# Three short moves in the opening of a fused attention-and-gated-MLP kernel

## The chip, the cores and the metric

The kernel runs on one core of a Trainium2 chip. Its metric is the device time in microseconds (us) of that core. A core has several engines that run side by side, each working through its own list of instructions in order: TensorE (PE in the profile, with its weight loads as PEld), VectorE (DVE), ScalarE (ACT), GpSimd (POOL) and SyncE (SP), which here issues every transfer (DMA). An engine waits for another through semaphores. TensorE writes only into PSUM, of which this kernel uses eight banks; a bank must be emptied by ScalarE or VectorE before TensorE may fill it again.

## The reference, cut to what matters

The input x has 2048 tokens of width 640. It is normalised once, and two branches read the result: a linear attention of 32 heads of width 20 and a gated MLP of width 1536.

```python
xn = (x - mean) / sqrt(var + 1e-5)
q, k, v = split(xn @ wqkv)                       # 32 heads of 20
pq, pk = q @ w_phi[h], k @ w_phi[h]              # per head
phi_q = concat(softmax(pq), softmax(-pq)); phi_k = concat(softmax(pk), softmax(-pk))
kv = phi_k.T @ v; z = sum(phi_k)
o = (phi_q @ kv) / (phi_q @ z + 1e-6)
out = x + o @ wo + (silu(xn @ w1) * (xn @ w3)) @ w2
```

## The kernel before, in words

Tokens are cut into 16 tiles of 128. `xnT` holds the normalised x transposed, the form in which TensorE needs it. The whole order is written out by hand: the kernel is a list of calls, and each engine gets its instructions in the order in which the calls come. This document is about the opening, the calls from line 683 to line 814; after them come 16 turns of `phi_unit` for k, then 20 turns for q with the output.

**Normalisation.** `stats(t, 2)` (L644) gives VectorE four `bn_stats` (L223) and two `bn_aggr` (L226) for two tiles, and GpSimd a chain of six small instructions (L233, L236, L255 to L261) that makes 1/sqrt(var) in `rstd`. `lx(t, 2)` (L649) has VectorE apply it (L265), and `by_dma(t)` (L677) has SyncE transpose a tile into `xnT` (L678). Tiles 0, 1 and 3 are transposed by TensorE instead (`T`, `by_pe`: five transposes at L283 into a bank, two copies by ScalarE at L287).

**Raw V.** For tiles 0 to 3 the product with V's weights starts before their statistics are there: `raw_part` (L294) multiplies unnormalised x. The result is emptied from PSUM with the factor `rstd`: `raw_scaled` does it on ScalarE in two activations (L305), `raw_scaled_dve` on VectorE in two `tensor_scalar` (L312). The rest of V comes from `V(t)`: ten matmuls (L344), three copies by ScalarE (L359).

**MLP units.** `unit()` makes ten matmuls of 512 columns, five for the gate (gp, weights w1) and five for up (weights w3), and ScalarE's tanh (L455). It returns a function which, when called, has VectorE form the two products: `gs` (L472), which frees the gate's bank, and the one into `reg_h` (L475), which frees up's. The units of the opening are g0 to g7. g0 and g1 are done in halves of 256 columns (`glu_half`, L461), since tiles 2 and 3 come later than 0 and 1. "Unit seven" is g6, the seventh of them.

**Fused weights.** k is never formed: `FB(d)` (L669) multiplies a chunk of k's weights, which SyncE has brought in transposed (`ldT`, L138), with phi's weights (`fuse`, six matmuls at L428, two copies by ScalarE at L437). phi's weights are first spread into blocks, `wphi`, by one VectorE product (`phi_blocks`, L419).

**PSUM.** Six banks are handed out singly (`bank`), in the order in which they come free; two form a pair (`two`). A call that takes a bank waits until the instructions that read its last content are done. Before the change `FB` takes the pair for even d and two single banks for odd d.

Of the kernel before, what the change touches and what calls it, by code (L numbers as in the profile page):

```python
# [12 lines left out]
def kernel(  # L13
# [17 lines left out]
    nc = tc.nc  # L31
# [3 lines left out]
    ALU = mybir.AluOpType  # L35
    AX = mybir.AxisListType

    _, S, D = A_x.shape
# [13 lines left out]
    CH = 6 * 3 * Dh  # L52
# [16 lines left out]
    def bank(name, dt=f32):  # L69
        n = 512 if dt == f32 else 1024  # L70
        return psum.tile([P, n], dt, name=name, tag="bank")
# [6 lines left out]
    wkphi = one.tile([P, KD, D], bf, name="wkphi")  # L78
# [17 lines left out]
    wkT, wqT, wv = w_nat[:, 0], w_nat[:, 1], w_nat[:, 2]  # L96
# [19 lines left out]
    v_raw = one.tile([P, RAW, D], f32, name="v_raw")  # L116
# [7 lines left out]
    def ld(dst, src):  # L124
        nc.sync.dma_start(out=dst, in_=src)  # L125
# [9 lines left out]
    with tc.manual_schedule():  # L135
        def ldT(dst, i, d):
            rows = slice(d * P, (d + 1) * P)
            nc.sync.dma_start_transpose(  # L138
                out=dst[:, :, rows], in_=A_wqkv[rows, i * D : (i + 1) * D]
            )  # L140
# [3 lines left out]
        def ld_tiles(t, n):  # L144
            ld(
                xin[:, (t // 4) % 3, t % 4 : t % 4 + n],
                x2[t * P : (t + n) * P, :].rearrange("(t p) d -> p t d", p=P),
            )
# [7 lines left out]
        for c in range(KD):  # L156
# [15 lines left out]
            out=mask[:], in_=mask[:], pattern=[[8, KD], [-20, 8]], base=0,  # L172
# [3 lines left out]
            out=mask[:], in_=mask[:], pattern=[[-8, KD], [20, 8]], base=19,  # L176
# [7 lines left out]
            out=own[:], in_=own[:], pattern=[[-64, 2], [-20, 3]], base=0,  # L184
# [3 lines left out]
            out=own[:], in_=own[:], pattern=[[64, 2], [20, 3]], base=19,  # L188
# [26 lines left out]
        rstd = one.tile([P, NST], f32, name="rstd")  # L215

        def ln_stats(*ts):
            made = []
            for t in ts:
                xt = xin[:, (t // 4) % 3, t % 4, :]  # L220
                st = work.tile([P, 2, 6], f32, name="st")
                for i in range(2):
                    nc.vector.bn_stats(out=st[:, i, :], in_=xt[:, i * HD : (i + 1) * HD])  # L223
                made.append(st)
            for t, st in zip(ts, made):
                nc.vector.bn_aggr(out=mv[:, t, :], in_=st[:])  # L226
# [4 lines left out]
        def ln_pow(t, n):  # L231
            r = slice(t, t + n)
            nc.gpsimd.tensor_scalar(  # L233
                out=ve[:, r], in0=mv[:, r, 1], scalar1=EPS, scalar2=None, op0=ALU.add
            )
            nc.gpsimd.tensor_tensor(out=ry[:, r], in0=ve[:, r], in1=mhalf[:, 0:n], op=ALU.pow)  # L236
# [8 lines left out]
        def ln_newton(t, n):  # L245

            r = slice(t, t + n)
            eng = nc.gpsimd
            if n == 1:
                eng.tensor_scalar(  # L250
                    out=rstd[:, r], in0=ry[:, r], scalar1=ve[:, r], scalar2=ry[:, r],
                    op0=ALU.mult, op1=ALU.mult,
                )
            else:
                eng.tensor_mul(out=rstd[:, r], in0=ry[:, r], in1=ry[:, r])  # L255
                eng.tensor_mul(out=rstd[:, r], in0=rstd[:, r], in1=ve[:, r])
            eng.tensor_scalar(
                out=rstd[:, r], in0=rstd[:, r], scalar1=-0.5, scalar2=1.5,
                op0=ALU.mult, op1=ALU.add,
            )  # L260
            eng.tensor_mul(out=rstd[:, r], in0=rstd[:, r], in1=ry[:, r])  # L261

        def ln_x(t):
            xt = xin[:, (t // 4) % 3, t % 4, :]
            nc.vector.tensor_scalar(  # L265
                out=xt, in0=xt, scalar1=mv[:, t, 0:1], scalar2=rstd[:, t : t + 1],
                op0=ALU.subtract, op1=ALU.mult,
            )
# [34 lines left out]
        def raw_scaled(t, ps):  # L303
            for i, (a, b) in enumerate(((0, CH), (CH, D))):
                nc.scalar.activation(  # L305
                    out=v_raw[:, t, a:b], in_=ps[i][:, 0 : b - a],
                    func=AF.Identity, scale=rstd[:, t : t + 1],
                )

        def raw_scaled_dve(t, ps, i):  # L310
            a, b = ((0, CH), (CH, D))[i]
            nc.vector.tensor_scalar(  # L312
                out=v_raw[:, t, a:b], in0=ps[i][:, 0 : b - a],
                scalar1=rstd[:, t : t + 1], scalar2=None, op0=ALU.mult,
            )

        def column_sum(c):
            junk = work.tile([P, D], bf, name="junk")
# [16 lines left out]
        def tile_of(t):  # L335
            return slice(t * P, (t + 1) * P)
# [81 lines left out]
        def phi_blocks():  # L418
            nc.vector.tensor_mul(  # L419
                out=wphi[:],  # L420
                in0=wps[:, :, None, :].to_broadcast([P, KD, 8, Dh]),
                in1=mask[:, :, :, None].to_broadcast([P, KD, 8, Dh]),
            )

        def fuse(dst, wT, d, ps):

            for b, c, h0, h1 in PARTS:
                nc.tensor.matmul(  # L428
                    ps[b][:, Dh * (h0 - 16 * b) : Dh * (h1 - 16 * b)],
                    wT[:, c, d * P : (d + 1) * P],  # L430
                    wphi[:, c, h0 - 6 * c : h1 - 6 * c, :],
                    start=((b, c) in ((0, 0), (1, 2))),
                    stop=((b, c) in ((0, 2), (1, 4))),
                    skip_group_check=True,
                )
            for b in range(2):
                nc.scalar.copy(out=dst[:, d, b * HD : (b + 1) * HD], in_=ps[b][:, 0:HD])  # L437

        def glu_unit(sc, fi, banks=None):

            gp, up = banks or (bank("gp")[:], bank("up")[:])
            for ps, w in ((gp, w1), (up, w3)):
                for c in range(KD):
                    nc.tensor.matmul(  # L444
                        ps,
                        w[:, c, fi * P : (fi + 1) * P],
                        xnT[:, c, sc * 512 : (sc + 1) * 512],
                        start=(c == 0),
                        stop=(c == KD - 1),
                    )  # L450
            return glu_done(sc, fi, gp, up)
# [6 lines left out]
        def glu_half(i, w, sc, fi, ps):  # L458

            for c in range(KD):  # L460
                nc.tensor.matmul(  # L461
                    ps[:, i * 256 : (i + 1) * 256],
                    w[:, c, fi * P : (fi + 1) * P],
                    xnT[:, c, sc * 512 + i * 256 : sc * 512 + (i + 1) * 256],
                    start=(c == 0),
                    stop=(c == KD - 1),
                    skip_group_check=True,
                )
# [175 lines left out]
        def stats(t0, n):  # L644
            ln_stats(*range(t0, t0 + n))
            ln_pow(t0, n)
            ln_newton(t0, n)

        def lx(t0, n):  # L649
            if t0 < BY_DMA:  # L650
                nc.vector.reciprocal(out=rstd[:, t0 : t0 + n], in_=ry[:, t0 : t0 + n])
            for t in range(t0, t0 + n):
                ln_x(t)
# [3 lines left out]
        T = x_transposed  # L657

        def unit(banks=None):
            return glu_unit(*glu.pop(0), banks)  # L660

        def two(name):
            both = pair(name)
            return both[:, 0], both[:, 1]

        def V(t, ps=None):
            v_unit(vaug[:, t], tile_of(t), ps)

        def FB(d):  # L669
            if d % 2:  # L670
                ps = [bank("pf"), bank("pf")]
            else:
                ps = two("pf")
            fuse(wkphi, wkT, d, ps)


        def by_dma(t):  # L677
# [12 lines left out]
        vps = [two("v0"), [bank("pv"), bank("pv")]]  # L690
# [26 lines left out]
        ld_glu(256, 512)  # L717
        ld_tiles(8, 2)
        ld_tiles(10, 2)
        raw_scaled(1, vps[1])  # L720
        lx(3, 1)
        raw_scaled_dve(0, vps[0], 0)
        raw_scaled_dve(0, vps[0], 1)
        ps2 = [bank("pv"), bank("pv")]
        for c in range(KD):
            raw_part(2, c, ps2)
        ps3 = [bank("pv"), bank("pv")]
        for c in range(KD):
            raw_part(3, c, ps3)
        T(3)  # L730
        (sc, fa), (_, fb) = glu.pop(0), glu.pop(0)
        ga, ua = two("g0")
        glu_half(0, w1, sc, fa, ga)
        raw_scaled(2, ps2)
        raw_scaled(3, ps3)
        gb = bank("gp")[:]
# [49 lines left out]
        by_dma(12)  # L786
        by_dma(13)
        V(8)
        stats(14, 2)
        V(9, two("pv"))  # L790
        phi_blocks()
        V(10)
        V(11, two("pv"))
        ldT(wkT, 1, 2)
        lx(14, 2)
        by_dma(14)
        by_dma(15)
        ldT(wkT, 1, 3)
        ldT(wkT, 1, 4)
        g6 = unit()  # L800
        FB(0)
        g6()
        V(12)
        FB(1)
        ld_glu(512, F)
        nc.sync.dma_start_transpose(out=wqT, in_=A_wqkv[:, 0:D])
        V(13)
        g7 = unit()
        g7()
        FB(2)  # L810
        V(14)
        FB(3)
        FB(4)
        V(15)

# [111 lines left out]
```

## Time and profile before

| what | value |
|---|---|
| median of 3 runs | 270.81 us (270.58 to 270.89) |
| the profiled execution's own time | 270.84 us |
| its span, first to last instruction | 269.1 us |
| TensorE busy | 262.1 us, 97% |
| VectorE, ScalarE, GpSimd busy | 192.6, 115.2, 91.9 us |
| TensorE's granted clock | full speed in every slice |

The span is 1.7 us shorter than the execution's time; that rest lies around the program. In a row of the timeline stand the start, the length, the engine, the line, the operation with its output and inputs, how many instructions were merged, and in brackets how long the engine had been idle before and for whom. Matmuls are pipelined: each row's length contains the last matmul's run through the array, so that the distance from one start to the next tells what a group costs.

### The profile page before, as it was taken

Reading aid. Unit: us, or ns where it says so; the run is one execution under the profiler, and the core shown is the slowest. Engines: PE = TensorE matmul, PEld = TensorE weight load, DVE = VectorE, ACT = ScalarE, POOL = GpSimd, SP = SyncE. Lnnn points to the kernel's source line nnn. Section 1 sums busy time; section 2 is a strip of 40 time slices with the busy share of each in tenths; the row PEclk is TensorE's granted clock in tenths of the full one; section 3 lists DMA queues with packets and bytes.
Section 4 is the critical chain, followed back from the end, with each engine's and each line's share of the span. In section 5 each row is a group of like instructions: output and inputs, shape, how many; then the busy total and the mean of one; then the engine's idle time right before and its main releaser. Section 6 shows DMA issues by size and latency. Waiting matters only on the chain.

```text
span 269.1 us, 5283 instructions
## 1 busy us (share of the span) xinstructions
PE 262.1 (97%) x1977; PEld 167.2 (62%) x1996; DVE 192.6 (72%) x360; ACT 115.2 (43%) x350; POOL 91.9 (34%) x89
## 2 busy tenths in 40 slices
PE   8999998999999999999999999999999999999994
PEld 6666565655555555555555555677777777777773
DVE  4698964297777777779997789977667777776341
ACT  5774455745566665435665555422222222221000
POOL 5052530064333333424543333333344444333000
PEclk9999999999999999999999999999999999999999
DMA  6988555995000000060000296556554655556831
GB/s 182 254 229 171 101 121 100 345 199 94 0 0 2 0 1 3 1 173 0 0 2 0 54 307 74 120 139 148 130 136 119 151 129 127 140 140 129 153 97 55
DMA packets 67660, 29.11 MB, mean 108 GB/s; under 512 B 54576, under 2 KB 66224, under 8 KB 67632
## 3 DMA queue, kind: packets, MB, share of 16 engines
q1 hardware_dynamic: 67632, 28.74, 45.2%
q8 instruction: 17, 0.28, 0.4%
q14 instruction: 11, 0.09, 0.2%
HBM read 13.13 MB, written 2.62 MB: 59 GB/s over the span
## 4 chain that ended last, share of the span: by engine, by line
PE 83%; DVE 9%; POOL 3%; DMA 2%; issue 2%; SPq 1%; DVEq 0%
PE acc L583 27%; PE up L444 16%; PE gp L444 16%; PE pq L344 8%; PE pk L344 8%; DVE st L223 3%; PE pr L520 2%; PE pkv L485 2%; DMA reg_h<-in_A_x_dram 2%; DVE reg_h L265 2%; DVE reg_h L475 2%; PE pv L344 2%; DVE gs L472 1%; SPq L125 1%; POOL ry L236 1%
## 5 line engine op out<-in xcount | busy, mean ns | idle before, releaser
L410 POOL TENSOR_TENSOR phi<-phi,rk 128x1320 bf16<-128x1320 bf16 x32 | 77.3, 2414 | 130.6 <-DVE rk L409 96.9
L444 PEld LDWEIGHTS <-w 128*128 128x128 bf16 x460 | 43.5, 98 | 48.3 <-DMA w<-in_B_w_dram 0.5
L407 DVE TENSOR_REDUCE sk<-phi 128x66 f32<-128x1320 bf16 x32 | 48.8, 1527 | 30.7 <-ACT phi L373 29.6
L444 PE MATMUL up<-xnT,w 128*128 128x512 bf16 x226 | 56.8, 379 | 0.3
L444 PE MATMUL gp<-xnT,w 128*128 128x512 bf16 x215 | 56.0, 378 | 0.7
L583 PE MATMUL acc<-reg_v,reg_h 128*128 128x320 bf16 (+2 forms) x384 | 54.9, 299 | 0.0
L344 PEld LDWEIGHTS <-xnT 128*128 128x128 bf16 x440 | 41.8, 98 | 19.9 <-issue 1.1
L373 ACT ACTIVATE phi<-pq 128x360 bf16<-128x360 f32 (+2 forms) x96 | 24.8, 364 | 58.0 <-issue 53.9
L583 PEld LDWEIGHTS <-reg_h 128*128 128x128 bf16 x384 | 37.3, 98 | 14.4
L455 ACT ACTIVATE th<-gp 128x512 f32<-128x512 f32 x47 | 28.3, 602 | 30.0 <-PE gp L444 29.5
L475 DVE SCALAR_TENSOR_TENSOR reg_h<-gs,up 128x512 bf16<-128x512 bf16 x47 | 32.3, 688 | 5.2 <-DVE gs L472 0.5
L373 ACT ACTIVATE phi<-pk 128x360 bf16<-128x360 f32 (+2 forms) x96 | 24.8, 364 | 20.7 <-PE pk L344 20.7
L472 DVE SCALAR_TENSOR_TENSOR gs<-th,gp 128x512 bf16<-128x512 f32 x47 | 30.9, 658 | 3.2 <-ACT th L455 3.2
L592 DVE TENSOR_TENSOR res<-acc,xr 128x320 bf16<-128x320 f32 (+2 forms) x32 | 14.3, 487 | 19.8 <-PE acc L583 19.8
L583 PE MATMUL acc<-reg_w,reg_v 128*128 128x320 bf16 (+2 forms) x160 | 24.5, 299 | 0.0
L344 PE MATMUL pk<-wkphi,xnT 128*128 128x360 bf16 (+1 forms) x160 | 24.3, 299 | 0.0
L344 PE MATMUL pq<-wqphi,xnT 128*128 128x360 bf16 (+1 forms) x160 | 24.3, 299 | 0.0
L409 DVE RECIPROCAL rk<-sk 128x66 f32<-128x66 f32 x32 | 18.1, 567 | 3.2
L583 PEld LDWEIGHTS <-reg_v 128*128 128x128 bf16 x160 | 15.7, 98 | 6.1
L344 PE MATMUL pv<-reg_w,xnT 128*128 128x360 bf16 x120 | 17.4, 299 | 0.8 <-DVE reg_h L475 0.5
L223 DVE BATCH_NORM_STATS2 st<-reg_h 128x6 f32<-128x320 bf16 x32 | 13.4, 477 | 4.2 <-DMA reg_h<-in_A_x_dram 4.2
L541 DVE TENSOR_TENSOR o__77<-pr,den 128x360 bf16<-128x360 f32 (+1 forms) x32 | 14.2, 486 | 0.6
(79 smaller groups left out, 159.0 us busy)
## 6 DMA issues: line engine op xcount, KB each, us to landing
w<-in_B_w_dram SPq DMA_DIRECT2D x2, 1280.0 KB, 8.7
xr<-in_A_x_dram SPq DMA_DIRECT2D x16, 160.0 KB, 2.5
out_dram<-res SPq DMA_DIRECT2D x15, 160.0 KB, 1.8
reg_h<-in_A_x_dram SPq DMA_DIRECT2D x6, 320.0 KB, 4.5
reg_v<-in_B_w_dram SPq DMA_DIRECT2D x1, 1920.0 KB, 8.8
w<-in_B_w_dram SPq DMA_DIRECT2D x4, 320.0 KB, 4.7
reg_w<-in_A_wqkv_dram SPq DMA_DIRECT2D x5, 160.0 KB, 3.8
reg_w<-in_A_wo_dram SPq DMA_DIRECT2D x1, 800.0 KB, 7.7
```

Source lines behind the costliest of these rows:

```text
L223: nc.vector.bn_stats(out=st[:, i, :], in_=xt[:, i * HD : (i + 1) * HD])
L344: nc.tensor.matmul(ps[i][:, 0 : b - a], xnT[:, c, cols], w[:, c, a:b], start=(c == 0), stop=(c == KD - 1), skip_group_check=True,)
L373: nc.scalar.activation(out=dst[:, c0 : c0 + n, g, 0:k], in_=p.rearrange("p (c f) -> p c f", c=n), func=AF.Exp, scale=1.0 - 2.0 * g,)
L407: nc.vector.reduce_sum(out=sk[:], in_=rows, axis=AX.X)
L409: nc.vector.reciprocal(out=rk[:], in_=sk[:])
L410: nc.gpsimd.tensor_mul(out=rows, in0=rows, in1=rk[:, :, :, None].to_broadcast([P, 2 * NCH, 3, Dh]))
L444: nc.tensor.matmul(ps, w[:, c, fi * P : (fi + 1) * P], xnT[:, c, sc * 512 : (sc + 1) * 512], start=(c == 0), stop=(c == KD - 1),)
L455: nc.scalar.activation(out=th[:], in_=gp, func=AF.Tanh, scale=0.5)
L472: nc.vector.scalar_tensor_tensor(out=gs[:], in0=th[:], scalar=1.0, in1=gp, op0=ALU.add, op1=ALU.mult)
L475: nc.vector.scalar_tensor_tensor(out=hT[:, 4 * sc : 4 * sc + 4, fi, :], in0=gs[:].rearrange("p (t s) -> p t s", t=4), scalar=0.5, in1=up.r ...
L583: nc.tensor.matmul(ps[:, 0 : b - a], rows[j][0], rows[j][1][:, a:b], start=(j == 0), stop=(j == len(rows) - 1),)
L592: nc.vector.tensor_tensor(out=res[:, a:b], in0=ps[:, 0 : b - a], in1=xr[:, a:b], op=ALU.add)
```

## The change

1. `raw_scaled_dve` goes. Raw V of tile 0 is now emptied by ScalarE (`raw_scaled(0, vps[0])`), ahead of tile 1's. VectorE has two instructions less there, ScalarE two more.
2. `T(3)`, the transposes of tile 3 on TensorE, moves behind the first half of g0's gate.
3. `phi_blocks` moves ahead of `stats(14, 2)` and of `V(9)`.
4. g6 and its products move ahead of `lx(14, 2)` and of the transposes of tiles 14 and 15. `ldT(wkT, 1, 3)` moves ahead of those transposes as well.
5. `FB` always takes the pair. `FB(2)` moves ahead of g7, and `FB(3)` ahead of `V(14)`, so that no two `FB` follow each other directly.

```diff
-        def raw_scaled_dve(t, ps, i):
-            a, b = ((0, CH), (CH, D))[i]
-            nc.vector.tensor_scalar(
-                out=v_raw[:, t, a:b], in0=ps[i][:, 0 : b - a],
-                scalar1=rstd[:, t : t + 1], scalar2=None, op0=ALU.mult,
-            )
...
         def FB(d):
-            if d % 2:
-                ps = [bank("pf"), bank("pf")]
-            else:
-                ps = two("pf")
-            fuse(wkphi, wkT, d, ps)
+            fuse(wkphi, wkT, d, two("pf"))
...
+        raw_scaled(0, vps[0])
+        lx(3, 1)
         raw_scaled(1, vps[1])
-        lx(3, 1)
-        raw_scaled_dve(0, vps[0], 0)
-        raw_scaled_dve(0, vps[0], 1)
...
-        T(3)
         (sc, fa), (_, fb) = glu.pop(0), glu.pop(0)
         ga, ua = two("g0")
         glu_half(0, w1, sc, fa, ga)
+        T(3)
         raw_scaled(2, ps2)
...
         V(8)
+        phi_blocks()
+        V(9, two("pv"))
         stats(14, 2)
-        V(9, two("pv"))
-        phi_blocks()
         V(10)
         V(11, two("pv"))
         ldT(wkT, 1, 2)
+        ldT(wkT, 1, 3)
+        g6 = unit()
+        g6()
         lx(14, 2)
         by_dma(14)
         by_dma(15)
-        ldT(wkT, 1, 3)
         ldT(wkT, 1, 4)
-        g6 = unit()
         FB(0)
-        g6()
         V(12)
         FB(1)
         ld_glu(512, F)
         nc.sync.dma_start_transpose(out=wqT, in_=A_wqkv[:, 0:D])
         V(13)
+        FB(2)
         g7 = unit()
         g7()
-        FB(2)
+        FB(3)
         V(14)
-        FB(3)
         FB(4)
         V(15)
```

## The prediction

> **What bounds the kernel.** I read the page's busy shares and slices first.
>
> ```profile
> span 269.1 us, 5283 instructions
> PE 262.1 (97%) x1977; PEld 167.2 (62%) x1996; DVE 192.6 (72%) x360; ACT 115.2 (43%) x350; POOL 91.9 (34%) x89
> PEclk9999999999999999999999999999999999999999
> ```
>
> TensorE is busy from end to end at full clock, so a change can only gain where TensorE stands still. Second, whom TensorE waited for, whole span:
>
> ```profile
> PE idle L200 <- DVE nought L196: 1.1, 1, 1.1
> PE pv L344 <- DVE reg_h L475: 0.5, 1, 0.5
> PE v L294 <- DMA reg_w<-in_A_wqkv_dram: 0.4, 1, 0.4
> PE pv L344 <- DVE gs L472: 0.3, 1, 0.3
> PE g L461 <- DVE v_raw L312: 0.2, 1, 0.2
> ```
>
> That is the whole list. The change touches three of these: the two pv waits and the g wait. From 43 us to the end the same view is empty, so what TensorE gains by then should reach the end. Third, the timeline of TensorE around the pv waits:
>
> ```profile
> 39.00 0.48 PE L428 MATMUL pf<-wphi,reg_w 128*128 128x140 bf16 x6
> 39.32 1.52 PE L344 MATMUL pv<-reg_w,xnT 128*128 128x360 bf16 x10
> 40.67 0.48 PE L428 MATMUL pf<-wphi,reg_w 128*128 128x140 bf16 x6
> 41.48 0.31 PE L344 MATMUL pv<-reg_w,xnT 128*128 128x360 bf16 x1 [0.33 <-DVE gs L472]
> 42.27 1.37 PE L344 MATMUL pv<-reg_w,xnT 128*128 128x280 bf16 x9 [0.48 <-DVE reg_h L475]
> 43.47 1.24 PE L444 MATMUL gp<-xnT,w 128*128 128x512 bf16 x5
> ```
>
> By starts, an FB costs 0.32 (39.00 to 39.32) and a V 1.35 (39.32 to 40.67). FB(1) and V(13) should take 1.67 and took 2.80 (40.67 to 43.47). V(13) was handed g6's two banks, and VectorE freed them late. Why late, fourth, from VectorE, GpSimd and SyncE:
>
> ```profile
> 28.89 0.22 POOL L233 TENSOR_SCALAR ve<-mv 128x2 f32<-128x2 f32 x1 [3.57 <-DVE mv L226]
> ...
> 37.08 0.94 DVE L419 TENSOR_TENSOR wphi<-wps,mask 128x800 bf16<-128x800 bf16 x1
> 37.25 0.84 POOL L233 TENSOR_SCALAR ve<-mv 128x2 f32<-128x2 f32 x1 [4.04 <-DVE mv L226]
> ...
> 40.03 0.80 DVE L265 TENSOR_SCALAR reg_h<-reg_h,mv,rstd 128x640 bf16<-128x640 bf16 x2 [2.01 <-POOL rstd L261]
> 40.74 0.68 DVE L472 SCALAR_TENSOR_TENSOR gs<-th,gp 128x512 bf16<-128x512 f32 x1
> 41.53 0.69 DVE L475 SCALAR_TENSOR_TENSOR reg_h<-gs,up 128x512 bf16<-128x512 bf16 x1
> ```
>
> VectorE idled 2.01 us for GpSimd's rstd of tiles 14 and 15, with g6's products queued behind, although their tanh had ended at 38.72. Fifth, the g wait at 12.85 and the next wait for weights:
>
> ```profile
> 12.85 0.71 PE L461 MATMUL g<-xnT,w 128*128 128x256 bf16 x5 [0.19 <-DVE v_raw L312]
> ...
> 17.32 0.76 PEld L444 LDWEIGHTS <-w 128*128 128x128 bf16 x5 [0.22 <-DMA w<-in_B_w_dram]
> ```
>
> **The change part by part.**
>
> *g6's products ahead of lx(14).* They start after the tanh, at 38.8, and take 1.48 as before (40.74 to 42.22): done by 40.28. V(13)'s turn on TensorE comes at 40.67 + 0.32 = 40.99, so even g6's own banks are free, by 0.7. With FB(1) on the pair V(13) takes an older set, V(10)'s, copied out by 36.4. Gain: 2.80 - 1.67 = **1.13**.
>
> *phi_blocks ahead of stats(14).* The statistics end 0.87 later (0.94 less the overlap with its neighbour), so GpSimd starts at 38.12. Its chain took 2.12 when ve took 0.22 (28.89 to 31.01) and 2.75 beside wphi (37.25 to 40.00); at 38.12 wphi is done, so I take 2.12: rstd at 40.24, against 40.00. lx(14) follows there, when g6's products are just over, 0.24 later than before. FB(0), which reads wphi, stands at 39.00. The Trainium skill (SBUF — State Buffer, Who interferes with whom) says that a VectorE instruction with two SBUF inputs contends with a GpSimd instruction that reads SBUF. The trace agrees: ve stood 0.84, up to wphi's end, and POOL's other waits before a ve (3.57) left it at 0.22. Without that rule 2.75 would stand, and the transfers below would come 0.63 later, a cost of up to 0.7.
>
> *SyncE.* ldT(2) was issued at 38.05; ldT(3) now follows, to 40.64. The transpose of tile 14 starts 0.24 later than its 40.50, at 40.74, tile 15's at 42.03, ldT(4) at 43.31 (was 44.39). Tiles land 2.4 after issue, so 14 and 15 lie in xnT at 43.2 and 44.5; V(14) and V(15) read them at 45.1 and 46.8. ldT's took 2.8 to 3.2 to land, so chunk 4 is there at 46.1 to 46.5. The later loads of w1 and w3 start about 0.4 earlier.
>
> *FB on the pair.* Each FB now waits for ScalarE's copies of the one before. New starts on TensorE: FB(1) 40.67, V(13) 40.99, FB(2) 42.34, g7 (2.16) 42.66, FB(3) 44.82, V(14) 45.14, FB(4) 46.49, V(15) 46.81. FB(0)'s copies ended at 40.27. FB(1)'s ended at 42.24 and follow V(12)'s, which do not move: 0.1 before FB(2). FB(2)'s and FB(3)'s have 2 and 1 us. FB(4)'s binding wait is chunk 4: cost 0 to 0.06. Before, that chunk held FB(4) by 0.03 (landed 47.62, due 47.63 with its load ahead, started 47.66). I take 0 now, a gain of 0.03; the upper end is 0.7 if SyncE runs as late as in the sentence on 2.75.
>
> *Raw V of tile 0 on ScalarE, T(3) moved.* Two activations cost 0.93 (the row at 10.91 for tile 1), VectorE sheds 1.00. ScalarE empties tile 0 by 11.84, before TensorE wants the pair, at 12.22. Five transposes take 0.27, so g could have begun at 12.49 and began at 12.85: 0.36 lost before. The eight halves of 0.545 then end at 16.85 instead of 17.21. But g2's w1 landed at 17.28 and it began at 17.32; its load was issued behind tile 2's transpose, and nothing ahead of it on SyncE moves. So the 0.36 becomes a wait for w1: gain **0**. It would be a gain if w1 landed earlier.
> ScalarE itself: tile 3's copies start 0.48 after its transposes, at 13.25 instead of 12.70, so tiles 2 and 3 and the table load run 0.55 later and g0's tanh ends at 17.69. VectorE took it up at 17.60, so its first product is 0.15 late; lx(6) had waited to 19.09 for rstd, 0.08 past the product's end and a usual 0.08 of overlap, which covers it. That rstd comes 0.6 earlier, since the statistics of 4 and 5 start 0.95 sooner and those of 6 and 7 at their landing, 13.95. If the cover fails, 0.55 goes down VectorE's chain to lx(10): tile 10 landed at 33.9 and V(10) began at 34.12, so the cost is at most 0.35. A loss is not excluded; I take 0.
> The transposes of tiles 4 and 5 go out 1 us earlier, at 16.4, while w3's quarter is landing (18.31, wanted 18.41). Landings followed the order of issue throughout the opening, so I take 0. Upper end: their 320 KB ahead of w3 at the window's 243 GB/s, 1.3 less 0.1 slack, 1.2.
>
> **Sum.** 1.13 + 0.03 + 0 = 1.16. The profiled execution took 270.84, 0.03 over the median: 269.68, and 269.65 beside the median; I say **269.7**, or 0.4% faster.
>
> **The rivals.**
> 1. *Part of it comes back*: chunk 4 late at FB(4), or VectorE's lateness at V(10). Their margins, 0 and 0.2, are the smallest here; against it stands that both shifts come out near zero. Cost 0.2 to 0.7: 269.9 to 270.4.
> 2. *The opening gains too.* The profile names VectorE's v_raw as what released tile 2's transpose on SyncE, whose issue took 2.25 against the usual 1.2. If removing v_raw shortened it by 1.0, w1 would land at 16.3 and 0.4 more could be won, of which V(10)'s tile leaves 0.2: 269.4. Against: that issue began at 11.29, right when its input was ready, and 640 KB issued before it were landing until 13.95. The Trainium skill (the same section) says that DMA never contends with a compute engine except through GpSimd's descriptors; by it this rival falls, and no other row here shows it.
> 3. *No change*: w3 comes late by the 1.2 above, and TensorE waits at 18.4 what it wins at 41: 270.9.
> 4. *Slower: the round of banks in the pk turns.* Which freed bank comes next is not written in the kernel, and FB(1) and FB(3) no longer take four. In the turn at 58.5 to 64.5 the first unit's product ended at 65.08; a pk that got that unit's banks would wait from 64.54 to 65.13, 0.59 a turn. Two such turns eat the gain, three give 271.5, sixteen 279. For it: this is how V(13) lost 1.13. Against: all takes are by twos, as before, so that a set returns after three takes, and TensorE waited in none of these turns.
>
> **How the numbers follow.** The forecast, 269.4 to 269.9, gets 0.66; rival 1 0.10 (0.08 of it beyond 0.2%), rival 2 0.06, rival 3 0.06, rival 4 0.12, where I leave room for anything that I have not seen and that costs. 0.2%, 0.54 us, is about what a measurement of this kernel can tell from no change. Faster: 0.66 + 0.06 + 0.08 = 0.80; same: 0.02 + 0.06 = 0.08; slower 0.12. From 269.3 to 270.4 lie the forecast and rivals 1 and 2, 0.82.
>
> **What would show it.** After: no wait of pv on g6's products; VectorE's two products before L265's last pair, whose idle time is short; ve at 0.22 in the chain of tiles 14 and 15; from FB(1)'s start to pk's first matmul 7.5 (8.68 before); the g wait gone and PEld's wait for w1 at 17.3 grown to about 0.6; no waits of TensorE after 48. Wrong would be: a wait of pf on copies or on the transposes, pv waiting for xnT at 34, PEld waiting for w3 past 18.4, or waits of pk or gp in the turns.

## The result and the profile after

The kernel after the change takes **269.08 us** (268.99 to 269.30, 5 runs) against 270.58 (270.21 to 270.89, 5 runs) for the kernel before in the same session: a ratio of 0.9947, with a 95% interval of 0.9935 to 0.9959. That is faster, by 0.5%, and clear of the noise. The forecast was 269.7 with a range from 269.3 to 270.4: the sign and the mechanism of the late part were right, a gain in the beginning was put at nothing, and the median lies 0.2 below the low end. Two of the executions reported below, one of e2 at 562.48 us and one of e10 at 278.42, were slow ones and enter their medians but no ratio.

The profiled execution took 269.18 us, its span 267.4. The page's first lines:

```profile
span 267.4 us, 5287 instructions
PE 261.9 (98%) x1977; PEld 167.8 (63%) x1996; DVE 192.1 (72%) x358; ACT 116.1 (43%) x352; POOL 91.2 (34%) x89
PEclk9999999999999999999999999999999999999999
```

TensorE has the same work (261.9 against 262.1) in a shorter span. Whom it waited for, whole span; the columns are engine, line, releaser, then total us, times and longest:

```profile
PE idle L200 <- DVE nought L196: 1.1, 1, 1.1
```

One line is left, the start of the program. Both pv waits and the g wait are gone, and so is the wait for a weight load at the start of raw V (0.4), which comes and goes between executions. Lines after the removed function have numbers lower by 7 to 12. TensorE's timeline in the late part of the opening:

```profile
38.46 0.48 PE L421 MATMUL pf<-wphi,reg_w 128*128 128x140 bf16 x6
38.78 1.52 PE L337 MATMUL pv<-reg_w,xnT 128*128 128x360 bf16 x10
40.13 0.48 PE L421 MATMUL pf<-wphi,reg_w 128*128 128x140 bf16 x6
40.45 1.52 PE L337 MATMUL pv<-reg_w,xnT 128*128 128x360 bf16 x10
41.81 0.48 PE L421 MATMUL pf<-wphi,reg_w 128*128 128x140 bf16 x6
```

FB(1) and V(13) now take 1.68 (40.13 to 41.81), where they took 2.80. VectorE and GpSimd at the same time:

```profile
37.60 0.22 POOL L233 TENSOR_SCALAR ve<-mv 128x2 f32<-128x2 f32 x1 [4.95 <-DVE mv L226]
...
38.21 0.69 DVE L465 SCALAR_TENSOR_TENSOR gs<-th,gp 128x512 bf16<-128x512 f32 x1 [0.70 <-ACT th L448]
39.00 0.69 DVE L468 SCALAR_TENSOR_TENSOR reg_h<-gs,up 128x512 bf16<-128x512 bf16 x1
39.74 0.80 DVE L265 TENSOR_SCALAR reg_h<-reg_h,mv,rstd 128x640 bf16<-128x640 bf16 x2
```

g6's two products stand ahead of the normalisation of tiles 14 and 15, which starts without idle time, and `ve` is 0.22. Now the beginning, TensorE's matmuls and the loads of g2's first weights:

```profile
12.16 0.71 PE L454 MATMUL g<-xnT,w 128*128 128x256 bf16 x5
12.70 0.44 PE L283 MATMUL pst<-ident,reg_h 128*128 128x128 bf16 x5
...
16.69 4.09 PEld L437 LDWEIGHTS <-w 128*128 128x128 bf16 x20
16.80 1.24 PE L437 MATMUL gp<-xnT,w 128*128 128x512 bf16 x4
```

g's first half starts 0.69 earlier than before (12.85): 0.36 is the wait for v_raw, 0.27 the transposes that now follow, 0.06 an earlier arrival. g2 starts at 16.80 instead of 17.32. Its weights are loaded at 16.69 without idle time before, so no wait for w1 has taken the place of the g wait. That is where the forecast failed.

How far TensorE is ahead of the profile of before, read at starts in the two traces:

| at | before | after | ahead by |
|---|---|---|---|
| the second matmul group of g0 (gp) | 13.40 | 12.98 | 0.42 |
| g2 | 17.32 | 16.80 | 0.52 |
| FB(0) | 39.00 | 38.46 | 0.54 |
| pk's first matmul | 49.35 | 47.63 | 1.72 |
| end of the span | 269.1 | 267.4 | 1.7 |

So 0.5 of these two traces' 1.7 comes before 17 us, 1.2 between FB(0) and pk, and nothing is lost or won afterwards. (pk's first matmul to the end takes 219.77 to 219.79 in all fourteen traces of this document.)

### The profile page after: what moved, and what is told of

It reads as the page before. It is cut to its first block, busy times and chain, and to the rows that moved or that the text cites. A ratio compares the mean times of both kernels' runs of the same rounds, so it can differ in the third digit from the quotient of the medians.

```text
span 267.4 us, 5287 instructions
## 1 busy us (share of the span) xinstructions
PE 261.9 (98%) x1977; PEld 167.8 (63%) x1996; DVE 192.1 (72%) x358; ACT 116.1 (43%) x352; POOL 91.2 (34%) x89
## 4 chain that ended last, share of the span: by engine, by line
PE 98%; issue 0%; DVE 0%
PE acc L576 28%; PE up L437 19%; PE gp L437 18%; PE pq L337 8%; PE pk L337 8%; PE pv L337 6%; PE pr L513 2%; PE pkv L478 2%; PE pv L294 2%; PE pf L421 1%; PE idle L200 1%; PE pst L283 1%; PE g L454 1%; PE v L294 1%; PE gp L454 0%
```

## The experiments

All ratios are to the kernel before, on the same chip in the same session; a gain in us is that ratio's distance from 1, times the session's median of before (270.45, 270.44 or 270.22).

### The two halves of the change apart

**e1_late_only**: the kernel before with parts 3, 4 and 5 of the change; the beginning untouched.

```diff
+        phi_blocks()
         V(9, two("pv"))
         stats(14, 2)
...
+        ldT(wkT, 1, 3)
+        g6 = unit()
+        g6()
         lx(14, 2)
...
+            fuse(wkphi, wkT, d, two("pf"))
...
```

> The kernel before with the second half of the change alone (phi_blocks, g6, ldT(3) and FB moved; the opening as before). By the prediction's sum V(13) no longer waits (1.13) and FB(4) no longer waits for its chunk (0.03): 1.16 us faster, the wait of g for VectorE's v_raw at 12.85 and the wait for w1 at 17.3 both still there. If instead the whole measured gain of 1.5 belongs to the late stage, this kernel is 1.5 faster.

Measured: 269.44 (268.98 to 269.53, 5 runs); ratio 0.9958 (0.9946 to 0.9971), a gain of 1.14 (0.78 to 1.46). The late part is worth what the forecast's sum of 1.16 gave it. The two waits that were to remain did not show in this trace: w1 landed at 16.05, and g lost 0.11 by starts and lists no wait. What that means comes below.

**e2_opening_only**: the kernel before with parts 1 and 2 alone.

```diff
+        raw_scaled(0, vps[0])
         lx(3, 1)
-        raw_scaled_dve(0, vps[0], 0)
-        raw_scaled_dve(0, vps[0], 1)
+        raw_scaled(1, vps[1])
...
-        T(3)
...
         glu_half(0, w1, sc, fa, ga)
+        T(3)
```

> The kernel before with the opening's part alone (raw V of tile 0 on ScalarE, T(3) moved). By the prediction: g no longer waits, but TensorE then waits for w1 until 17.3, 0 us gained. By the rival that w1 lands 1.0 earlier once VectorE's v_raw is gone: tile 2's transpose on SyncE takes 1.2 to 1.3 to issue and w1 lands near 16.3. The second unit then starts near 16.85, but V(13) still waits for VectorE, whose lx(14) follows GpSimd, so what is won at 17 is partly lost at 41: between 0 and 0.5 faster.

Measured: median 270.31, 12 runs; ratio 0.9989 (0.998 to 0.9998), a gain of 0.30 (0.05 to 0.54). TensorE's waits in it:

```profile
PE idle L200 <- DVE nought L196: 1.1, 1, 1.1
PE pv L344 <- DVE reg_h L475: 0.5, 1, 0.5
PE pv L344 <- DVE gs L472: 0.3, 1, 0.3
```

The g wait is gone, the pv waits stand as before. The forecast had put these two parts at 0. The two halves add up: 1.14 + 0.30 = 1.44, and the whole change gave 1.43 by its ratio (0.0053 times 270.58). With intervals of some 0.3 on each side, so close an agreement is luck.

### Which of the late moves carries the gain

**e3_g6_first**: the kernel before with only g6 and its products ahead of `lx(14, 2)`.

```diff
         ldT(wkT, 1, 2)
+        g6 = unit()
+        g6()
         lx(14, 2)
...
         ldT(wkT, 1, 4)
-        g6 = unit()
         FB(0)
-        g6()
```

> The kernel before with g6 and its products ahead of lx(14), nothing else (FB on pair and single banks in turn, ldT(3) behind the transposes of tiles 14 and 15). If the late products are all that holds the stage, V(13) starts at 40.99 and the kernel is 1.1 faster. If the transposed weights are the next bound, chunk 4 still lands near 47.6 and FB(4), due at 46.5, waits about 1.1 for it: within 0.15 of no change.

Measured: 270.64, 13 runs; ratio 1.0005 (0.9996 to 1.0013): no change. The pv waits went, but TensorE's timeline shows a new one:

```profile
47.37 0.48 PE L428 MATMUL pf<-wphi,reg_w 128*128 128x140 bf16 x6
48.70 0.49 PE L428 MATMUL pf<-wphi,reg_w 128*128 128x140 bf16 x6 [0.86 <-DMA reg_w<-in_A_wqkv_dram]
```

FB(4) waits 0.86 for chunk 4 of k's weights. SyncE's own timeline tells why:

```profile
39.05 1.27 SPq L138 DMA_TRANSPOSE reg_w<-in_A_wqkv_dram  x1
41.81 2.52 SPq L678 DMA_TRANSPOSE xnT<-reg_h  x2
44.38 2.59 SPq L138 DMA_TRANSPOSE reg_w<-in_A_wqkv_dram  x2
```

With `ldT(3)` and `ldT(4)` still behind the transposes of tiles 14 and 15, which wait for the last normalisation, both chunks are issued from 44.38 on; chunk 4 landed at 48.66. (In this execution x's tile 2 landed at 9.56 instead of 8.53, which moved TensorE and SyncE alike by some 1.1.)

**e4_pair_only**: the kernel before with only the pair for `FB` and the new order of `FB(2)` and `FB(3)`.

```diff
-            if d % 2:
-                ps = [bank("pf"), bank("pf")]
-            else:
-                ps = two("pf")
-            fuse(wkphi, wkT, d, ps)
+            fuse(wkphi, wkT, d, two("pf"))
...
         V(13)
+        FB(2)
         g7 = unit()
         g7()
-        FB(2)
-        V(14)
         FB(3)
+        V(14)
```

> The kernel before with FB always on the pair and FB(2), FB(3) moved forward, nothing else (g6's products still behind lx(14)). V(13) then takes V(10)'s banks and does not wait. If banks are all that holds the stage: 1.1 faster. If the transposed weights are the next bound, FB(3), due at 44.8, waits for chunk 3 (landed 45.96) and FB(4) for chunk 4 (47.62): within 0.15 of no change.

Measured: 270.41, 12 runs; ratio 0.9999 (0.9991 to 1.0008): no change. TensorE's timeline:

```profile
40.82 1.52 PE L344 MATMUL pv<-reg_w,xnT 128*128 128x360 bf16 x10
42.17 0.48 PE L428 MATMUL pf<-wphi,reg_w 128*128 128x140 bf16 x6
...
45.48 0.49 PE L428 MATMUL pf<-wphi,reg_w 128*128 128x140 bf16 x6 [0.67 <-DMA reg_w<-in_A_wqkv_dram]
```

V(13) no longer waits, with g6's products as late as before: it was handed other banks. But FB(3), one step earlier in the list, waits 0.67 for chunk 3, which landed at 45.44.

**e9_g6_and_ldT** and **e10_pair_and_ldT**: e3 and e4, each with `ldT(wkT, 1, 3)` moved ahead of `lx(14, 2)` as well. The line that e9 adds to e3, and e10 to e4:

```diff
         ldT(wkT, 1, 2)
+        ldT(wkT, 1, 3)
...
         by_dma(15)
-        ldT(wkT, 1, 3)
         ldT(wkT, 1, 4)
```

> The kernel before with g6 and its products and ldT(3) ahead of lx(14), nothing else. If chunk 4 was what ate the gain of g6 alone: ldT(4) is issued near 43.3 instead of 45.7, lands near 46.3, FB(4) waits under 0.1 and the kernel is 1.0 to 1.2 faster. If it was something else: no change, as with g6 alone.

> The kernel before with FB on the pair, its new order and ldT(3) ahead of lx(14), g6's products left behind lx(14). If chunks 3 and 4 were what ate the gain: FB(3) and FB(4) do not wait and the kernel is 1.0 to 1.2 faster, with g6's products as late as before. If g6's products must come early as well: no change.

Measured: e9 269.47 (269.01 to 269.72, 7 runs), ratio 0.9961 (0.9947 to 0.9976), a gain of 1.05; e10 median 269.62, 12 runs, ratio 0.9963 (0.9951 to 0.9976), a gain of 1.0. Neither shows a wait of TensorE after 35 us. VectorE's timeline of e10:

```profile
39.98 0.81 DVE L265 TENSOR_SCALAR reg_h<-reg_h,mv,rstd 128x640 bf16<-128x640 bf16 x2 [2.00 <-POOL rstd L261]
40.70 0.68 DVE L472 SCALAR_TENSOR_TENSOR gs<-th,gp 128x512 bf16<-128x512 f32 x1
41.49 0.69 DVE L475 SCALAR_TENSOR_TENSOR reg_h<-gs,up 128x512 bf16<-128x512 bf16 x1
```

VectorE still idles its 2.00 us and frees g6's banks as late as ever, and the gain is there all the same. So the late gain needs two things: the transfer of chunk 3 earlier on SyncE, with which chunk 4 follows earlier too, and *either* g6's products earlier *or* other banks for V(13). Either of the last two alone uncovers the chunks. The earlier chunk alone was not run. All fourteen traces agree: FB(0) to pk takes 9.17 in the nine that have both things, and 9.95 to 10.35 in the five that lack one or both (before, e2, e3, e4, e13).

**e11_phi_blocks_back**: the kernel after with `phi_blocks` at its old place behind the last statistics.

```diff
         V(8)
-        phi_blocks()
-        V(9, two("pv"))
         stats(14, 2)
+        V(9, two("pv"))
+        phi_blocks()
```

> The changed kernel with phi_blocks back behind stats(14). If wphi's product holds GpSimd's ve: ve takes 0.8 to 0.9 again instead of 0.22, rstd of 14 and 15 still comes 0.2 to 0.3 earlier than in the changed kernel, and lx(14) follows g6's products either way: the time is the changed kernel's, within 0.15 us. If moving phi_blocks carried part of the gain: slower than the changed kernel by over 0.3.

Measured: 269.36 (269.00 to 269.72, 6 runs); ratio 0.9966 (0.9953 to 0.9979), a gain of 0.92 in a session in which before stood at 270.22. That is 0.5 less than the change's 1.43 in another session, more than was expected; the intervals of the two ratios overlap, and the one execution of after in the same session (e14) took 269.75. So the times alone don't settle it. GpSimd and VectorE in its trace:

```profile
36.58 0.84 POOL L233 TENSOR_SCALAR ve<-mv 128x2 f32<-128x2 f32 x1 [4.04 <-DVE mv L226]
...
39.48 0.80 DVE L265 TENSOR_SCALAR reg_h<-reg_h,mv,rstd 128x640 bf16<-128x640 bf16 x2
```

`ve` is back at 0.84, but the normalisation still follows directly on g6's products, without idle time. The trace has a span of 267.3, as short as that of after, and takes as long from FB(0) to pk (9.17). Once those products stand ahead, rstd is early enough either way; the move of `phi_blocks` carries nothing that these traces can tell.

### Why the beginning gained

The forecast held that g's wait would turn into a wait for w1, whose load is queued on SyncE behind the transpose of tile 2. Rival 2 held that VectorE's emptying of raw V had lengthened that transpose's issue. A third explanation came from the traces: a block of TensorE's instructions, fetched on queue 8, is in flight just then. The transfers of the kernel before in the window from 11.3 to 13.2 us (queue and kind: packets, MB, share of the 16 engines):

```profile
q1 hardware_dynamic: 713, 0.33, 107.4%
q8 instruction: 1, 0.02, 4.8%
```

**e7_raw_on_dve**: the kernel after with raw V of tile 0 back on VectorE; `T(3)` stays at its new place.

```diff
-        raw_scaled(0, vps[0])
-        lx(3, 1)
         raw_scaled(1, vps[1])
+        lx(3, 1)
+        raw_scaled_dve(0, vps[0], 0)
+        raw_scaled_dve(0, vps[0], 1)
```

> The changed kernel with raw V of tile 0 back on VectorE behind lx(3); T(3) stays behind the first half of g0. If VectorE's v_raw holds g: TensorE waits about 0.6 before g (from 12.2 to 12.8, no T(3) in between), and the time is 0.3 to 0.6 above the changed kernel's, 0.9 to 1.2 faster than before. If the opening is held by w1's landing anyway: as fast as the changed kernel. Tile 2's transpose on SyncE takes 1.2 to 1.3 to issue if the fetch starts over 1.0 after it, about 2 if earlier, and not because of v_raw.

**e12_T3_old_place**: the kernel after with `T(3)` back ahead of g0's first half; raw V stays on ScalarE.

```diff
+        T(3)
         (sc, fa), (_, fb) = glu.pop(0), glu.pop(0)
         ga, ua = two("g0")
         glu_half(0, w1, sc, fa, ga)
-        T(3)
```

> The changed kernel with T(3) back ahead of the first half of g0; raw V of tile 0 stays on ScalarE. If emptying tile 0 earlier is what the opening gains by: no wait of g, the time is the changed kernel's within 0.2 us. If T(3)'s place is what counts: g or T(3) waits 0.1 to 0.4 and the time is up to 0.4 above the changed kernel's.

**e5_fetch_later**: the kernel after, with its 19 warm-up matmuls and their weight loads replaced by five wider ones. TensorE has 28 instructions less, 14 matmuls and 14 loads, so that every block of instructions should fall due later. The warm-up computes nothing that is used.

```diff
-        warm(WARM)
+        for _ in range(5):
+            nc.tensor.matmul(
+                idle[:], nought[:], nought[:, None, :].to_broadcast([P, 4, P])
+            )
```

> The changed kernel, with the 19 warm-up matmuls of 128 columns replaced by 5 of 512: about the same warm-up time, 28 instructions fewer on TensorE's list ahead of the opening. Theory 1 (SyncE's issue stands still while a block of TensorE's instructions is fetched on queue 8): the first fetch, seen between 11.6 and 12.9 us so far, comes 1.5 us or more later; tile 2's transpose takes 1.2 to 1.3 us to issue and w1's load after it 0.5 to 0.6 (1.07 in the changed kernel's trace), and the issue that is then under the fetch is the stretched one. Theory 2 (VectorE's work or the backlog of loads stretches it): the stretched issue stays that of tile 2 or w1, wherever the fetch goes. Time: like the changed kernel's, within 0.3 us, since TensorE waits for nothing there.

**e13_before_again** and **e14_after_again**: both kernels unchanged, one execution each, for the spread between executions of one kernel.

> The kernel before, unchanged, for a second trace of it. If w1's landing at 17.3 and the 2.25 us issue of tile 2's transpose belong to the kernel, both return. If they are chance (where the fetch of TensorE's instructions falls against that issue), the issue takes 1.3 when the fetch starts over 1.0 after it, and w1 lands near 16.5; g's wait for VectorE, 0.2, and V(13)'s two waits return in any case.

> The changed kernel, unchanged, for a second trace of it. Neither V(13) nor FB waits. If the issue of tile 2's transpose falls under the fetch this time, it takes about 2 us, w1 lands near 17 and TensorE waits up to 0.5 for it; if not, 1.3, w1 near 16.4 and no wait.

Measured times: e7 269.94, 12 runs, ratio 0.9978 (0.9968 to 0.9988), a gain of 0.6; e12 269.50, 8 runs, ratio 0.997 (0.9953 to 0.9988), a gain of 0.8; e5 270.11, 12 runs, ratio 0.9989 (0.9973 to 1.0004), a gain of 0.3; e13 270.62 and e14 269.75, one run each. e7 came out 0.8 below the gain of after, where 0.3 to 0.6 was expected; its trace lost 0.36 at g and 0.5 more later (see what stays open). What all fourteen traces show around the transpose of tile 2 (us; the fetch is the block on queue 8, the gap runs from the start of the issue to the start of the fetch; the landing of w1's load is its semaphore):

| trace | raw V of tile 0 on | issue starts | fetch | gap | issue takes | w1 lands |
|---|---|---|---|---|---|---|
| before | VectorE | 11.29 | 11.64–13.10 | 0.35 | 2.25 | 17.28 |
| e3 | VectorE | 12.32 | 12.70–13.88 | 0.38 | 2.05 | 18.08 |
| e7 | VectorE | 10.97 | 11.42–12.53 | 0.45 | 2.02 | 16.54 |
| e12 | ScalarE | 11.20 | 11.67–12.78 | 0.47 | 2.07 | 17.06 |
| e13 (before) | VectorE | 11.00 | 11.66–12.62 | 0.66 | 2.05 | 16.57 |
| e4 | VectorE | 10.86 | 11.65–12.90 | 0.79 | 2.48 | 17.11 |
| e10 | VectorE | 11.28 | 12.18–13.18 | 0.90 | 1.32 | 16.50 |
| e14 (after) | ScalarE | 11.24 | 12.15–13.30 | 0.91 | 1.32 | 16.61 |
| after | ScalarE | 10.80 | 11.82–12.88 | 1.02 | 1.32 | 16.28 |
| e11 | ScalarE | 10.63 | 11.68–12.94 | 1.05 | 1.32 | 16.10 |
| e2 | ScalarE | 11.00 | 12.10–13.10 | 1.10 | 1.32 | 16.39 |
| e9 | VectorE | 10.77 | 12.02–13.00 | 1.25 | 1.32 | 16.65 |
| e1 | VectorE | 10.38 | 11.67–12.66 | 1.29 | 1.32 | 16.05 |
| e5 | ScalarE | 10.95 | 13.26–14.41 | 2.31 | 1.32 | 16.44 |

Sorted by the gap, the table splits cleanly: with the fetch 0.79 or less behind, the issue takes 2.0 to 2.5; with 0.90 or more it takes 1.32. In each of the six long ones the issue ends 0.43 to 0.49 after the fetch. Which engine empties raw V does not decide it: three traces with VectorE have 1.32 (e1, e9, e10) and one with ScalarE has 2.07 (e12). SyncE's rows of e1 and then of e12, two of these four:

```profile
10.38 1.32 SPq L674 DMA_TRANSPOSE xnT<-reg_h  x1
11.76 1.85 SPq L125 DMA_DIRECT2D w<-in_B_w_dram  x2
```

```profile
11.20 2.07 SPq L667 DMA_TRANSPOSE xnT<-reg_h  x1
13.33 1.14 SPq L125 DMA_DIRECT2D w<-in_B_w_dram  x2
```

In e1 the fetch falls on the next instructions, the two loads of weights, and it is they that are stretched (1.85 against 1.14). It is so in all seven traces with a gap from 0.90 to 1.29: the first of the two, w1's, takes 0.89 to 1.28 to issue and ends 0.33 to 0.38 after the fetch; in the seven others it takes 0.57. In e5 the fetch came 1.4 us later than in the trace of after, and the stretch moved on once more, past the weights to the loads of tiles 8 to 11 (1.83, against 1.04 in the trace of before):

```profile
10.95 1.32 SPq L670 DMA_TRANSPOSE xnT<-reg_h  x1
12.32 1.14 SPq L125 DMA_DIRECT2D w<-in_B_w_dram  x2
13.50 1.83 SPq L125 DMA_DIRECT2D reg_h<-in_A_x_dram  x2
```

So e5 bears out the explanation as to the issue. As to the time, the expectation was missed: about 1 us worse than after. The fetch now ended at 14.41, tile 2 landed at 15.48, and TensorE waited for it.

```profile
15.52 1.25 PE L457 MATMUL g<-xnT,w 128*128 128x256 bf16 x10 [0.98 <-DMA xnT<-reg_h]
```

A long issue does not always make w1 late. Among the six long ones w1 lands 3.95 to 4.28 after the end of the fetch, so that with the two earliest fetches it came at 16.54 and 16.57 all the same (e7, e13; so e13 fits neither of the two cases set out for it). The four landings after 17 all belong to long issues; with short ones w1 landed between 16.05 and 16.65.

What it means for the kernel before: its profile, with w1 at 17.28, was one of the late ones. In e13, the same kernel once more, w1 landed at 16.57, and TensorE began g2 without a wait for it:

```profile
12.57 0.71 PE L461 MATMUL g<-xnT,w 128*128 128x256 bf16 x5
...
16.94 1.24 PE L444 MATMUL gp<-xnT,w 128*128 128x512 bf16 x4
```

In the four executions with the beginning of before and w1 at 16.05 to 16.65 (e1, e9, e10, e13), g2's weights were there before they were due, at 16.4 to 17.2, so that what g lost was not covered by a wait for w1. What it lost varies as well: by starts 0.36 and 0.35 in e10 and e9, 0.17 in e13, 0.11 in e1. Part 1 removes that. e7 shows the counterpart: raw V back on VectorE, and g waits again.

```profile
12.54 0.71 PE L461 MATMUL g<-xnT,w 128*128 128x256 bf16 x5 [0.36 <-DVE v_raw L312]
```

In e12, with a late w1 (17.06), g2 began at 17.11 where TensorE was ready at 16.90: there the wait for w1 that the forecast had expected did come, at 0.2. Of its two cases, e12 bears out the first: with `T(3)` at its old place g follows the transposes after 0.27 and does not wait, so it is the earlier emptying that removes the g wait. Its gain is 0.6 below the 1.43 of another session, more than was expected, but with an interval of almost 0.5 on each side that is not clear of the noise.

The starts of all traces also give the size of the gain in the beginning, free of when TensorE arrives there (11.57 to 13.25). Counted from the start of T(3) or of g, whichever comes first, g2 starts 4.64 or 4.65 later in after, e2, e11 and e14, and 4.80 to 5.10 later in the seven with the beginning of before; FB(0) starts 26.30 or 26.31 later against 26.65 to 26.94. So the beginning gains 0.35 to 0.64 by FB(0). e2's 0.30 to the end lies at the low side of that, its interval reaching 0.54; there V(13) still waits for VectorE. A single pair of traces can mislead here: e14, the kernel after once more, began g2 at 17.32, as late as the profile of before, since TensorE arrived 0.5 later.

## Why the prediction was right or wrong

**The failed step** is "nothing ahead of it on SyncE moves. So the 0.36 becomes a wait for w1: gain **0**." The landing of w1 at 17.28 was taken as fixed, from one execution. In fact it moves by 1.2 us between executions of kernels with the same beginning (16.05 in e1, 17.28 in before; e3, with its late tile 2, left out), and in the traces that goes with when SyncE's issue starts and when a block of instructions crosses it. In four of these six it comes before it is due, in e13 of the very same kernel too. For what g lost alone the term should have lain between 0 and 0.36, nearer the upper end; e2 measured 0.30 (0.05 to 0.54). The 0.52 between the two traces at g2 is 0.06 of arrival, the 0.36, and the 0.11 that the profile of before lost to its own late w1 (17.32 against 17.21).

**The miss in numbers.** The forecast beside the median was 269.65, the result 269.08, which is 0.57 less. 0.34 of it is gain (1.50 between the medians against 1.16). The other 0.23 is the base: three runs had a median of 270.81, the five beside the result 270.58. With the beginning's 0.30 in the sum the forecast would have been 269.35, and with the base as well 269.12, which leaves 0.04, far below what the intervals can tell.

**Point by point.**
- *g6's products ahead of lx(14), 1.13*: right in size. FB(1) and V(13) take 1.68 as forecast (1.67), and FB(1) to pk takes 7.50 (40.13 to 47.63), the forecast's number, against 8.68 before. e1's 1.14 (0.78 to 1.46) stands against 1.16. The 1.13 too was read from one execution, which was the dearest: FB(1) and V(13) took 2.77 in e2 and 2.46 in e13, where the same reckoning gives 1.10 and 0.79. The forecast saw that g6's order and the banks are each enough for V(13); it did not see that each is worth nothing without SyncE's change (e3, e4).
- *SyncE*: right that `ldT(3)` before the transposes brings the chunks in time. It was priced at 0.03 as a step of its own; e3 and e4 show that it carries the 1.0, in the sense that without it the gain is eaten at FB(4) or FB(3).
- *phi_blocks*: `ve` went from 0.84 to 0.22, as forecast from the row. The Trainium skill (SBUF — State Buffer, Who interferes with whom) says that a GpSimd instruction that reads SBUF contends with a VectorE instruction with two SBUF inputs. The traces agree: 0.84 in the eight with `wphi` beside it (before, e2, e3, e4, e9, e10, e11, e13) and 0.22 in the six without (after, e1, e5, e7, e12, e14). The loss of up to 0.7 priced for the case of 2.75 did not arise; e11, with `ve` at 0.84, shows that the normalisation is covered either way.
- *FB on the pair, 0*: right; no wait of pf on copies.
- *V(10)'s tile*: wrong for the changed kernel. Rival 2 let it leave only 0.2 of an earlier start. But tile 10's normalisation came earlier as well, at 30.49 instead of 31.04; the tile landed at 33.34 and V(10) began at 33.58, without a wait. With the old beginning the limit is real: in e13 tile 10 landed at 34.14 and V(10), due at 33.79, began at 34.18, which took back the 0.38 that g2 was ahead.
- *The waits to look for*: the g wait is gone, as said; PEld's wait for w1 did not grow to 0.6 but is gone; none after 48, as said.

**The rivals.** Rival 2's effect came, its cause did not: the opening gained, but neither from VectorE's v_raw on SyncE's issue nor with V(10) as the limit. That no compute engine held the transfer fits the rule of the Trainium skill cited there; what goes with the longer issue is itself a transfer, and the forecast was wrong to take that rule as an argument against the effect. Rivals 1, 3 and 4 did not show: no wait for chunk 4, none for w3 at 18.4, none of pk in the turns, and the distance won at pk (1.72) is the distance at the end (1.7).

**What stays open.** How often w1 comes late in the kernel before is not known from seven traces of its beginning, and so neither is how the beginning's gain splits between the g wait, w1 and tile 10. e7 lost about 0.5 in its trace at V(8) and V(10), whose tiles landed late (31.50 and 34.39); a later block of TensorE's instructions was in flight while tile 8 was on its way (27.98 to 29.46), but whether that is the cause was not followed up. Medians of before differ by up to 0.36 between sessions (270.22 to 270.58), and the gains carry intervals of 0.3 to 0.5 on each side; e11's and e12's distances from after, 0.3 and 0.4 by their medians, 0.5 and 0.6 by their gains, are not clear of that. That the fetch holds SyncE's issue is borne out by the coincidence in time in fourteen traces and by the shift in e5; by what mechanism, no run shows.

## What to carry to other kernels

Before a freed wait is written off against the next one, ask how fixed that next one is: a landing time read from one execution can move by a microsecond, and a second profile of the unchanged kernel would have shown it. When an engine is late for several reasons, follow each of its supplies: here the banks and the chunks of weights were due within 6 us of each other, and removing the delay at the banks alone gave nothing. An edit that looks like bookkeeping on a DMA queue can be what makes the visible edit pay.

## What the runs showed of the hardware

- A block of instructions for TensorE (one packet of 0.02 MB on queue 8) in flight while SyncE issues a transfer goes with a longer issue: 2.0 to 2.5 us instead of 1.32 for a transpose when the block starts 0.35 to 0.79 after it, 0.89 to 1.28 instead of 0.57 for the weight load behind when it starts later. In all fourteen traces the issue so stretched ends 0.33 to 0.49 after the block. Tile 2's transpose then lands 1.45 to 1.60 after the end of the fetch in thirteen traces, and 1.07 after it in e5.
- VectorE stands 0.51 or 0.52 us before g3's second product in all eight traces with the two VectorE instructions for raw V. In the six without them it stands 0.10 there, as before other such products; a pause of 0.10 is not printed in the row. The kernel before and then the kernel after, VectorE's timeline:

```profile
25.57 0.69 DVE L475 SCALAR_TENSOR_TENSOR reg_h<-gs,up 128x512 bf16<-128x512 bf16 x1 [0.52 <-DVE gs L472]
```

```profile
25.03 0.69 DVE L468 SCALAR_TENSOR_TENSOR reg_h<-gs,up 128x512 bf16<-128x512 bf16 x1
```

In the kernel before the profile names only VectorE's own first product as what ended the pause, and no instruction block is in flight during it (25.05 to 25.57); its cause stays open. Of the 0.55 by which tile 10's normalisation came earlier (31.04 to 30.49), 0.42 were gained here.
